# Attention for batches 1 to 3: the two heads' 64-token tiles packed into one 128-partition tile

## The chip, the cores and the metric

One core of a Trainium2 chip runs the whole program. The metric is the device time of one execution in microseconds (us); a comparison uses the median of several runs. The core has a matrix engine (TensorE, PE in the profile, its weight loads as PEld), VectorE (DVE), ScalarE (ACT), GpSimd (POOL) and SyncE (SP), which here only issues DMAs.

## The reference

Local causal attention and a memory readout are mixed by a gate, and two dense feed-forward layers follow. Shapes: B=4, H=8, S=576, D=64; tokens x model 2304 x 512, hidden width 2048.

```python
scores = scale * q @ k.T                      # causal mask
a = exp(scores - max); a /= a.sum() + 1e-9
local = a @ v
q_p = phi(q)                                  # where(x > 0, x, exp(x) - 1) + 1
mem_out = (q_p @ M_prev) / (q_p @ z_prev + 1e-6)
attn = g * mem_out + (1 - g) * local          # g = sigmoid(beta), one per head
x = attn as [B*S, H*D]
h = x @ w_in;   y = (s * relu(h)**2 + b) @ w_out
h2 = y @ w_in2; out = (h2 * tanh(softplus(h2))) @ w_out2
```

## The kernel before

The attention is cut into half units. A half unit is one batch, one pair of heads, and either the first 320 tokens (group `TA`) or the last 256 (group `TB`); `pair` emits its steps. There are 4 x 4 x 2 = 32 of them. In front of the 576 tokens stand 64 rows of zeros, so that the padded 640 tokens make five query tiles of 128. Group `TA` has tiles 0, 1 and 2; of tile 0 only 64 rows are real tokens.

For one half unit of `TA` in batches 1 to 3 (twelve of them) `pair` does this:

- SP issues one DMA for q with z (`qn`, or a place in `stage`), one per head for q and k transposed (`qk`), one for M and v (`vx`), and at the end one for the result.
- POOL takes min(q, 0) (L535), ACT the exponential (L536), DVE forms phi(q), its product with z and the sum per head and token (L537 to L539), gates and inverts it (L533, L541).
- PE makes the scores (L571), for each of tiles 0, 1, 2 and each head one matmul with 64 rows of the array, 128 columns of weights and 64, 192 or 320 moving columns. The two heads use the two halves of the rows. They are two steps of the plan: tiles 0 and 1 into one pair of PSUM banks, tile 2 into another.
- DVE adds the mask, takes the row's extreme and writes SBUF (L581, one per tile and head); POOL writes the memory part, phi(q) times the inverse norm, in front of the scores (L592, the same count); ACT takes the exponential with its row sum (L589, the same count).
- DVE gates and inverts the sums (L533, L610), and POOL scales the rows (L607, the same count; `E_NORM[False]` is 'PPPPD' and tiles 0 to 2 are all 'P').
- PE transposes P block by block (L630, 6 blocks a head, 12 in all), ACT copies them to SBUF (L635), and PE multiplies with M and v (L652: 128 rows, 64 weight columns a head, the two heads in the two halves of the columns; 384, 256 and 128 moving columns).
- ACT copies 320 columns out (L666), and SP stores them to `x_d`.

Every fp32 matmul shows as two weight loads and two matmuls in the trace; a transpose shows as one.

The order of all steps on all engines is written by `Plan`, a list scheduler: each step has an engine, a cost and a priority, and the plan simulates the engines with these costs and emits the steps in the order that comes out. Attention steps have priorities from 50 upward (7 more for each half unit) and go ahead of the first feed-forward layer, whose matmuls (L881 and L957, priorities from 500) fill PE's free time. DMAs that put derived weights aside (L825, L866, L868, priority 499) fill SP's. Two sets of input buffers (one in pool `at`, one in `stage`) let one half unit be loaded ahead. PSUM ring `a` has five banks. After the attention come the rest of layer 1 and then the second layer's blocks (L1112, L1185, L1188).

The lines that decide how PE is laid out for the scores and for P times v:

```python
nc.tensor.matmul(ps[k][i].t[:, a:a + hi - lo], qkt(t * P, P)[rows(i)], kt(lo, hi - lo)[rows(i)], start=True, stop=True)   # L571
nc.tensor.matmul(pv.t[rows(i), cols].rearrange("p (t q) -> p t q", q=P), vx()[:, i, c, :], PT[i].t[...], ...)             # L652
```

Of the kernel before, what the change touches and what calls it, by code (L numbers as in the profile page):

```python
# [9 lines left out]
F32 = mybir.dt.float32  # L10
F32R = mybir.dt.float32r
BF16 = mybir.dt.bfloat16
I32 = mybir.dt.int32
U32 = mybir.dt.uint32
AF = mybir.ActivationFunctionType
ALU = mybir.AluOpType
# [3 lines left out]
P = 128  # L20
MASKED = -1.0e30
HUGE = 3.0e38
TRUNC = -0.5 + 2.0 ** -13 - 2.0 ** -15
PE, ACT, DVE, POOL, DMA = range(5)
# [29 lines left out]
def act_us(n, extra=0):  # L54
    return 0.094 + 0.00083 * n + 0.093 * extra


def dve_us(n, fast=False):
    return 0.068 + (0.00052 if fast else 0.00104) * n


def pool_us(n):
    return 0.3 + 0.0013 * n
# [6 lines left out]
def two(s):  # L70

    s.two = True
    return s
# [119 lines left out]
class Plan:  # L193
# [29 lines left out]
    def add(self, engine, us, prio, f, r=(), w=(), after=(), keep=(), share=1.0):  # L223


        bufs = list({id(b): b for b in (*r, *w, *keep) if b.ring is not None}.values())
        new = [b for b in bufs if b.maker is None]
        waits = {id(s): s for b in r for s in b.writers}
        waits.update((id(s), s) for s in after)
        s = Step(engine, us, prio, f, list(waits.values()), bufs, new)  # L230
        s.share = share
        s.left = len(waits)
        for x in waits.values():
            x.next.append(s)
        for b in bufs:
            b.users += 1
            if b.maker is None:
                b.maker = s
            elif id(b.maker) not in waits:
                b.maker.next_start.append(s)  # L240
                s.left += 1
        for b in w:
            b.writers.append(s)
        self.steps.append(s)
        return s
# [114 lines left out]
def attention_then_two_ffn(ctx: ExitStack, tc: tile.TileContext, qk, qz, vm, beta,  # L360
# [3 lines left out]
    nc = tc.nc  # L364
    B, H = qk.shape[:2]
    NQ, D = qz.shape[3] - 1, qz.shape[4]
    SP = NQ * P
    S = SP - D
# [16 lines left out]
    SCALE = 1.0 / float(D) ** 0.5  # L385
    TA, TB = groups_all = tuple(range(3)), tuple(range(3, NQ))
    NONE = 5
    plan = Plan()
    add = plan.add
# [6 lines left out]
    ident = const.tile([P, P], F32, name="ident")  # L396
    make_identity(nc, ident)
    mask = const.tile([P, SP], BF16, name="mask")
# [3 lines left out]
    igate = const.tile([P, 2, H], F32, name="igate")  # L402
    sb = const.tile([P, 2], F32, name="sb")

    x_d = dram.tile([P, NCC, NT], F32, name="x_d")
# [9 lines left out]
    x_in = {(b, g): Buf() for b in range(B) for g in range(2)}  # L415
# [21 lines left out]
    small, att = ExitStack(), ExitStack()  # L437
    m1s = small.enter_context(tc.tile_pool(name="m1s", bufs=1))
    at = att.enter_context(tc.tile_pool(name="at", bufs=1, side="right"))
    m1t, m2a, m2c = [], [], []  # L440

    R = {}
# [22 lines left out]
    attention_steps = []  # L465
# [3 lines left out]
    def pair(b, p, prio, g, place=None, apart=False):  # L469
# [4 lines left out]
        def add(engine, us, f, r=(), w=(), keep=(), share=1.0):  # L474
            attention_steps.append(plan.add(engine, us, prio, f, r, w, keep=keep, share=share))
            return attention_steps[-1]
# [190 lines left out]
        c0 = b * S + q0  # L667
        add(DMA, 0.7, lambda: nc.sync.dma_start(x_d[:, p, c0:c0 + m], xs.t[:, :m]), [xs], [x_in[b, groups_all.index(g)]])


    W = {}

# [584 lines left out]
    n = len(plan.steps)  # L1257
# [3 lines left out]
    for x, a in zip(("qk", "qn", "vx"), (0, 832, 1344)):  # L1261
        R[x].homes(stage, [a], conversion_left)
    for b, p, g, prio in halves_[H:]:
        pair(b, p, prio, g)
    R["c1"] = Ring("c1").homes(stage, [2048 + 256 * i for i in range(4)], conversion_left).more(m1s, 1, conversion_left)
    c1_steps = {"in": {r: [] for r in range(NR)}, "out": {r: [] for r in range(NR)}}
    for r in range(NR):
# [23 lines left out]
    order1, n = [], 0  # L1291
    for i in range(len(seq)):
        order1.append((i, True))
        for k in range(n, len(seq)):
# [3 lines left out]
            n = k + 1  # L1298
    for i, begins in order1:
# [3 lines left out]
        if begins:  # L1303
# [5 lines left out]
            m = len(plan.steps)  # L1309
            halves[i] = first(j, fcs, at_, -1.0)  # L1310
            in_steps[fcs[0] // FPR] += [x for x in plan.steps[m:] if x.engine == PE]
        else:
            y_part(part, fcs, accs[part], *halves.pop(i), at_ + 0.01)
            out_steps[fcs[0] // FPR] += plan.steps[m0:]
            m = len(plan.steps)
# [18 lines left out]
    n = len(plan.steps)  # L1334
# [26 lines left out]
    n = len(plan.steps)  # L1361
# [76 lines left out]
```

## Time and profile before

| | |
|---|---|
| median of 3 runs | 956.82 us (955.77 to 958.04) |
| the profiled execution's own time | 956.4 us |
| its span, first to last instruction | 954.6 us |
| PE busy | 937.3 us, 98% |
| DVE, ACT, POOL busy | 776.0, 641.5, 220.7 us |
| granted TensorE clock | 1.00 nearly throughout |

The chain of work that ended last follows each step back to what released it. A busy share is an average over stages; the stretches show which engine binds where. Attention of batches 1 to 3 runs from about 77 to 311 us.

### The profile page before, as it was taken

The page shows a single profiled execution, that of the slowest core. Times are in us where ns is not written, and L with a number is a line of the kernel's source. Part 1 is how long each engine was busy: PE and PEld are TensorE (multiplying, and loading weights), DVE is VectorE, ACT ScalarE, POOL GpSimd, SP SyncE. Part 2 cuts the span into 40 slices and gives each one's busy share as a digit, 9 for nine tenths or more (in the row PEclk, how much of TensorE's full clock was granted, in tenths as well). Part 3 has the DMA queues.
Part 4 walks back from the last instruction along what each step waited for, and adds up shares of the span by engine and source line. Part 5 has one row for each costly group of instructions (what it writes and reads, how often), then busy time and mean ns, then how long its engine had stood idle before and what let it go on. Part 6 is the DMA issues. An engine that isn't in the chain of part 4 may idle for free.

```text
span 954.6 us, 19318 instructions
## 1 busy us (share of the span) xinstructions
PE 937.3 (98%) x6594; PEld 862.0 (90%) x6594; DVE 776.0 (81%) x1886; ACT 641.5 (67%) x1393; POOL 220.7 (23%) x377
## 2 busy tenths in 40 slices
PE   7899999999999999999999999999999999999998
PEld 6677788878788999888899999999999999999998
DVE  6999989899978787568658998889957799577874
ACT  6899878777777476889757865557634476344652
POOL 4635445577663000000023400000000000000000
PEclk9999999999999999999999999999999999999999
DMA  9976757999996789988885658885786655775545
GB/s 236 311 201 176 235 162 224 266 267 265 283 257 198 221 282 308 291 301 274 291 289 165 206 184 266 303 278 177 234 285 218 209 163 191 259 226 199 170 139 178
DMA packets 148339, 224.11 MB, mean 235 GB/s; under 512 B 15120, under 2 KB 122640, under 8 KB 141328
## 3 DMA queue, kind: packets, MB, share of 16 engines
q1 hardware_dynamic: 141408, 174.63, 59.4%
q0 software_dynamic: 6688, 48.24, 15.3%
q8 instruction: 52, 0.85, 0.4%
q14 instruction: 47, 0.39, 0.1%
q10 hardware_dynamic: 144, 0.00, 0.0%
HBM read 159.39 MB, written 63.44 MB: 233 GB/s over the span
## 4 chain that ended last, share of the span: by engine, by line
PE 79%; DVE 4%; ACT 2%; DMA 1%; issue 1%; POOL 0%; DVEq 0%; POOLq 0%
PE bank L1112 20%; PE bank L1185 19%; PE bank L881 12%; PE bank L957 12%; PE bank L1188 5%; PE bank L652 4%; PE bank L630 4%; PE bank L571 3%; DMA stage<-wi_sums_d 1%; DVE S L740 1%; DMA qn<-in_qz 0%; DVE g L1118 0%; DVE woh L740 0%; POOL Pt L607 0%; DVE g L1150 0%
## 5 line engine op out<-in xcount | busy, mean ns | idle before, releaser
L1112 PE MATMUL bank<-wi,woh 128*128 128x384 f32 x477 | 112.5, 334 | 0.0
L1112 PE MATMUL bank<-wi,wol 128*128 128x384 f32 x483 | 105.9, 335 | 0.8 <-DVE wil L1118 0.6
L1185 PE MATMUL bank<-wol,S 128*128 128x256 f32 x756 | 102.3, 283 | 0.0
L1185 PE MATMUL bank<-woh,S 128*128 128x256 f32 x756 | 101.9, 283 | 0.0
L1185 PEld LDWEIGHTS bank<-wol,S 128*128 128x128 f32 x756 | 96.2, 192 | 0.0
L1185 PEld LDWEIGHTS bank<-woh,S 128*128 128x128 f32 x756 | 95.9, 192 | 0.0
L1112 PEld LDWEIGHTS bank<-wi,wol 128*128 128x128 f32 x483 | 85.6, 188 | 1.6 <-DVE wil L1118 0.9
L1112 PEld LDWEIGHTS bank<-wi,woh 128*128 128x128 f32 x477 | 85.2, 188 | 0.4
L589 ACT ACTIVATE Pt<-Pt,mx 128x64 f32<-128x64 f32 (+4 forms) x152 | 82.6, 564 | 1.8 <-DVE mx L581 1.8
L635 ACT COPY PT<-bank 128x384 f32<-128x384 f32 (+2 forms) x160 | 68.2, 491 | 22.4 <-PE bank L630 15.0
L607 POOL TENSOR_SCALAR Pt<-Pt,rs 128x448 f32<-128x448 f32 (+3 forms) x100 | 65.7, 676 | 39.2 <-DVE rs L610 26.8
L592 POOL TENSOR_SCALAR Pt<-ex,nm 128x64 f32<-128x64 f32 x152 | 60.2, 419 | 63.1 <-DVE nm L541 35.4
L630 PE MATMUL bank<-ident,Pt 128*128 128x128 f32 x444 | 62.5, 275 | 6.1 <-DVE Pt L607 1.7
L630 PEld LDWEIGHTS bank<-ident,Pt 128*128 128x128 f32 x444 | 49.5, 140 | 11.2 <-issue 3.4
L581 DVE CUSTOM_DVE_ANT_0 Pt<-bank,mask 128x64 f32<-128x64 f32 (+3 forms) x152 | 50.5, 373 | 8.0 <-PE bank L571 5.7
L739 ACT CAST woh<-stage 128x1024 fp32r<-128x1024 f32 (+2 forms) x42 | 37.2, 885 | 27.4 <-PE bank L1112 17.9
L740 DVE TENSOR_TENSOR woh<-stage,woh 128x1024 fp32r<-128x1024 f32 (+2 forms) x42 | 42.7, 1018 | 13.8 <-ACT woh L739 13.7
L1125 POOL TENSOR_SCALAR woh<-woh,sb 128x384 f32<-128x384 f32 (+1 forms) x6 | 5.5, 916 | 183.3 <-ACT woh L1124 183.3
L739 ACT CAST S<-g 128x384 fp32r<-128x384 f32 x56 | 28.7, 513 | 27.2 <-PE bank L1185 19.2
L1092 POOL DMA_DIRECT2D woh<-wo_split_d x13 | 6.9, 530 | 156.2 <-DVE g L1150 76.4
L881 PE MATMUL bank<-xh,wi 128*128 128x256 f32 x256 | 42.5, 292 | 0.0
L957 PE MATMUL bank<-gl,woh 128*128 128x256 f32 x256 | 41.5, 288 | 0.0
(331 smaller groups left out, 2491.1 us busy)
## 6 DMA issues: line engine op xcount, KB each, us to landing
woh<-wo_split_d POOLq DMA_DIRECT2D x13, 1024.0 KB, 5.6
wol<-wi_split_d POOLq DMA_DIRECT2D x12, 1024.0 KB, 5.2
wol<-wo_split_d POOLq DMA_DIRECT2D x11, 1024.0 KB, 5.2
stage<-in_w_in SPq DMA_DIRECT2D x21, 512.0 KB, 5.6
stage<-in_w_out SPq DMA_DIRECT2D x19, 512.0 KB, 4.7
stage<-wi_d SPq DMA_DIRECT2D x24, 384.0 KB, 5.1
stage<-wo_d SPq DMA_DIRECT2D x18, 512.0 KB, 3.7
wo_split_d<-high SPq DMA_DIRECT2D x32, 256.0 KB, 4.6
```

What stands on the lines that cost most here:

```text
L581: nc.vector.tensor_tensor_reduce(at_t(i, t, D + lo, D + hi), x.t[:, a:a + hi - lo], mask[:, SP - w + lo:SP - w + hi], -SCALE, mx.t[:, i, t ...
L589: nc.scalar.activation(at_t(i, t, D, w + D), at_t(i, t, D, w + D), AF.Exp, bias=mx.t[:, i, t + k:t + k + 1], scale=-1.0, accum_out=rs.t[:, ...
L592: add(POOL, 0.33, lambda i=i, t=t: nc.gpsimd.tensor_scalar(at_t(i, t, 0, D), ex.t[:, i, t - lo_t, :], nm.t[:, i, t - lo_t:t - lo_t + 1], 1 ...
L607: (nc.vector if e == DVE else nc.gpsimd).tensor_scalar(x, x, r, *((None, ALU.mult) if e == DVE else (1.0, ALU.mult, ALU.mult)))
L630: nc.tensor.transpose(ps.t[:, x, :], at_t(i, t, c * P, (c + 1) * P), ident)
L635: (nc.vector.tensor_copy if dve else nc.scalar.copy)(PT[i].t[:, x:x + n], ps.t[:, :n])
L739: lambda: (nc.scalar.copy if e == ACT else nc.vector.tensor_copy)(t[0](0), src()), r, [t[2], half], after)
L740: lo = two(add(DVE, dve_us(n), prio, lambda: nc.vector.tensor_tensor(t[0](1), src(), t[0](0).bitcast(F32), op=ALU.subtract), [*r, half], [ ...
L881: nc.tensor.matmul(ph, w_at(nm, r, cc)[:, o:o + P], x_at(x, cc), start=(begin and part == 0 and cc == 0), stop=(part == 2 and cc == NCC - ...
L957: nc.tensor.matmul(acc[ec // per].t[:, (ec % per) * n:(ec % per + 1) * n], w_at(nm, fc // FPR, fc % FPR)[:, ec * P:(ec + 1) * P], t(x)[:, ...
L1112: nc.tensor.matmul(ps.t[:, :H2], w[i // 4].t[:, j, kk, at_], x[kk].t[:, k], start=begin and part == kk == 0, stop=part == 2 and kk == 1, s ...
L1185: nc.tensor.matmul(acc[t].t[:, :DH], s.t[:, j, t * P:(t + 1) * P], x.t[:, k, q % 4], start=q == part == 0, stop=q == NQ2 - 1 and part == 2)
```

## The change

The twelve half units of `TA` in batches 1 to 3 go to a new function, `leading`, in place of `pair`. It leaves out the 64 zero rows: the 64-token tiles of both heads become slot 0, one tile of 128 partitions (head 0 in partitions 0 to 63, head 1 in 64 to 127), and slots 1 to 4 are the two full tiles of each head. So there are five tiles where there were six. The scores are one step in three banks; slot 0's two matmuls take 64 rows and 64 weight columns each, and the six matmuls are issued in a new order. q and z come in four DMAs where there was one. P has 11 blocks to transpose, and P times M for slot 0 is a matmul of 64 moving columns a head. At the start three DVE copies and two GpSimd copies fill two small tables, `gates` and `step_`. `pair` still does all other half units.

```diff
+    gates = at.tile([P, 2, H // 2, 5], F32, name="gates")
+    nc.vector.tensor_copy(gates[:, :, :, 1:]..., igate...to_broadcast([P, H, 2, 2]))
+    step_ = at.tile([P, D], BF16, name="step")
+    for i in range(2):
+        x = slice(D * i, D * i + D)
+        nc.vector.tensor_copy(gates[x, :, :, 0], igate[x, :, i::2])
+        nc.gpsimd.tensor_copy(step_[x], mask[x, SP - P + D * i:SP - P + D * i + D])
...
+    def leading(b, p, prio):
+        n_q, n_s = 320, 5
+        slots = ((0, 64), *((q, w, i) for i in range(2) for q, w in ((64, 192), (192, 320))))
...
+        add(DMA, 0.5, lambda: nc.sync.dma_start(zq(4, 4)..., qz[b, hs, :, 2:4]...), w=[q_in])
+        for i in range(2):
+            add(DMA, 0.15, lambda i=i: nc.sync.dma_start(q_in.t[rows(i), :6 * D]...[:, :, 0], qz[b, 2 * p + i, D:, 0:2]), w=[q_in])
+        add(DMA, 0.25, lambda: nc.sync.dma_start(zq(1, 2), qz[b, hs, :, 0]...), w=[q_in])
...
+        for a, n in ((0, 1), (1, 4)):       # the product with z, in two instructions
...
+        bank = [Buf(R["a"], [P, 512]) for _ in range(3)]
+        where = [(2, 0), (0, 320), (0, 0), (1, 320), (1, 0)]
+        def mm():
+            for s, i in ((0, 0), (4, 1), (2, 0), (0, 1), (1, 0), (3, 1)):
+                (q0, w), (x, a), full = slots[s][:2], where[s], s > 0
+                nc.tensor.matmul(bank[x].t[:, a:a + w] if full else bank[x].t[rows(i), a:a + w],
+                                 qk_in.t[rows(i), q0:q0 + (P if full else D)], qk_in.t[rows(i), n_q:n_q + w],
+                                 start=True, stop=True, skip_group_check=not full)
+        add(PE, 0.03 + 576 * 0.00167, mm, [qk_in], bank, [*Pt, mx, rs], 1.0)
...
+        for s in (0, 1, 3, 2, 4):           # mask and extreme (DVE), memory part (POOL), exponential (ACT)
...
+        for s in (0, 1, 3, 2, 4):           # scaling, all on POOL
+            add(POOL, pool_us(w), lambda s=s, w=w: nc.gpsimd.tensor_scalar(...), ...)
...
+        for x, o, blocks in ((0, 0, [(0, 0), (1, 0), (1, 1)]), (1, 0, [(3, 0), (3, 1)]),
+                             (0, 3, [(2, c) for c in range(3)]), (1, 2, [(4, c) for c in range(3)])):
...
+            for c, k in ((0, 0), (0, 1), (1, 1), (2, 1)):    # P times M and v; k == 0 is slot 0, 64 columns
...
-        pair(b, p, prio, g)
+        if g == TA:
+            leading(b, p, prio)
+        else:
+            pair(b, p, prio, g)
```

## Rows read from the trace of the kernel before

**Rows 1.** The page's busy times, and the chain's shares by engine.
```profile
PE 937.3 (98%) x6594; PEld 862.0 (90%) x6594; DVE 776.0 (81%) x1886; ACT 641.5 (67%) x1393; POOL 220.7 (23%) x377
...
PE 79%; DVE 4%; ACT 2%; DMA 1%; issue 1%; POOL 0%; DVEq 0%; POOLq 0%
```

**Rows 2.** Busy us by stretch: PE, PEld, DVE, ACT, POOL; clock, DMA share, GB/s.
```profile
100.00:150.00 50.00, 47.47 (x384) 39.62 (x383) 46.00 (x134) 40.49 (x99) 25.61 (x39) 1.00 0.65 191
150.00:200.00 50.00, 49.95 (x407) 40.69 (x406) 43.72 (x146) 38.45 (x111) 29.58 (x55) 1.00 0.91 258
...
500.00:550.00 50.00, 49.06 (x279) 47.80 (x277) 45.90 (x88) 40.44 (x79) 20.05 (x20) 1.00 0.58 185
```

**Rows 3.** The chain of waits, 283 to 296 us: start, length, what.
```profile
283.88 0.47 PE bank L957 x4
...
285.15 1.29 PE bank L571 x12
286.44 1.45 PE bank L652 x12
287.89 0.67 PE bank L957 x4
288.56 1.97 PE bank L630 x18
```

**Rows 4.** Timeline of PE, 76.5 to 81.5 us: scores of one half unit in two groups.
```profile
77.04 0.82 PE L571 MATMUL bank<-qk 64*128 64x64 f32 x8
77.79 0.73 PE L881 MATMUL bank<-xl,wi 128*128 128x256 f32 x4
78.45 0.81 PE L571 MATMUL bank<-qk 64*128 64x320 f32 x4
79.19 2.17 PE L652 MATMUL bank<-PT,wih 128*64 128x256 f32 x20
```

**Rows 5.** Timeline of PE and its weight loads, narrow stretches around 285 to 287 us.
```profile
285.74 0.70 PE L571 MATMUL bank<-qk 64*128 64x320 f32 x4
...
286.01 0.44 PE L571 MATMUL bank<-qk 64*128 64x320 f32 x2
...
286.37 0.14 PEld L652 LDWEIGHTS bank<-PT,vx 128*64 128x64 f32 x2 [0.44 <-issue]
...
286.37 0.20 PEld L652 LDWEIGHTS bank<-PT,vx 128*64 128x64 f32 x4 [0.44 <-issue]
```

**Rows 6.** Groups by line and shape, 140 to 312 us: busy us, mean ns.
```profile
L592 POOL TENSOR_SCALAR Pt<-ex,nm 128x64 f32<-128x64 f32 x94 | 34.4, 389 | 32.9 <-DVE nm L541 17.9 <-PE bank L571 5.9 <-DVE nm L533 3.9
...
L607 POOL TENSOR_SCALAR Pt<-Pt,rs 128x64 f32<-128x64 f32 x20 | 9.7, 500 | 18.0 <-DVE rs L610 14.2 <-ACT Pt L589 2.8 <-ACT xs L666 1.0
...
L589 ACT ACTIVATE Pt<-Pt,mx 128x64 f32<-128x64 f32 x18 | 6.5, 384 | 0.0
...
L581 DVE CUSTOM_DVE_ANT_0 Pt<-bank,mask 128x64 f32<-128x64 f32 x37 | 7.3, 217 | 3.3 <-PE bank L571 3.1 <-POOL Pt L592 0.2
```

**Rows 7.** Timeline of DVE and of POOL, 6.3 to 9.5 us.
```profile
8.18 0.69 DVE L717 SCALAR_TENSOR_TENSOR stage<-stage 128x512 int32<-128x512 int32 x1 [0.93 <-ACT stage L713]
...
7.66 1.18 POOL L535 TENSOR_SCALAR ex<-wih 128x384 f32<-128x384 f32 x1 [4.30 <-DMA wih<-in_qz]
```

**Rows 8.** Timeline of SP's queue, 193 to 204 us: DMA issues.
```profile
197.08 0.44 SPq L514 DMA_DIRECT2D stage<-in_qz  x1
197.62 0.45 SPq L516 DMA_DIRECT2D qn<-in_qz  x1
...
198.64 0.46 SPq L866 DMA_DIRECT2D wi_resident_d<-wi  x1
```

**Rows 9.** Who waited for whom, 50 to 320 us: us in total, times, longest.
```profile
POOL ex L535 <- DMA qn<-in_qz: 8.8, 4, 4.2
```

**Rows 10.** Timeline of PE where the second layer begins: idle us before, releaser.
```profile
504.78 0.44 PE L1112 MATMUL bank<-wi,wol 128*128 128x384 f32 x1 [0.59 <-DVE wil L1118]
...
550.72 0.81 PE L1188 MATMUL bank<-S,woh 128*128 128x384 f32 x3 [0.82 <-DVE S L740]
```

More of the change, by code (lines that the diff above doesn't have):

```diff
@@ L439, in attention_then_two_ffn @@
     at = att.enter_context(tc.tile_pool(name="at", bufs=1, side="right"))
+    gates = at.tile([P, 2, H // 2, 5], F32, name="gates")
+    nc.vector.tensor_copy(gates[:, :, :, 1:].rearrange("p k a (h t) -> p (k a) h t", t=2),
+                          igate.rearrange("p k (a h) -> p (k a) h", h=2).unsqueeze(3).to_broadcast([P, H, 2, 2]))
+    step_ = at.tile([P, D], BF16, name="step")
[3 more added lines that the diff above has]
+        nc.gpsimd.tensor_copy(step_[x], mask[x, SP - P + D * i:SP - P + D * i + D])
     m1t, m2a, m2c = [], [], []
@@ L668, in pair, with add, rows, zq @@
         add(DMA, 0.7, lambda: nc.sync.dma_start(x_d[:, p, c0:c0 + m], xs.t[:, :m]), [xs], [x_in[b, groups_all.index(g)]])
+    def leading(b, p, prio):
+        def add(engine, us, f, r=(), w=(), keep=(), share=1.0):
+            attention_steps.append(plan.add(engine, us, prio, f, r, w, keep=keep, share=share))
+            return attention_steps[-1]
+        hs = slice(2 * p, 2 * p + 2)
+        n_q, n_s = 320, 5
+        slots = ((0, 64), *((q, w, i) for i in range(2) for q, w in ((64, 192), (192, 320))))
+        qk_in, q_in, v_in = Buf(R["qk"], [P, 2 * n_q]), Buf(R["qn"], [P, 8 * D]), Buf(R["vx"], [P, 6 * D])
+        def rows(i):
+            return slice(D * i, D * i + D)
+        def zq(a, n):
+            return q_in.t[:, a * D:(a + n) * D].rearrange("p (s d) -> p s d", d=D)
+        def q_all():
+            return zq(3, 5)
+        add(DMA, 0.5, lambda: nc.sync.dma_start(zq(4, 4).rearrange("p (h t) d -> p h t d", t=2), qz[b, hs, :, 2:4].rearrange("h p a d -> p h a d")), w=[q_in])
+        for i in range(2):
+            add(DMA, 0.15, lambda i=i: nc.sync.dma_start(q_in.t[rows(i), :6 * D].rearrange("p (k s d) -> p k s d", k=2, d=D)[:, :, 0],
+                                                         qz[b, 2 * p + i, D:, 0:2]), w=[q_in])
+        add(DMA, 0.25, lambda: nc.sync.dma_start(zq(1, 2), qz[b, hs, :, 0].rearrange("h p d -> p h d")), w=[q_in])
+        for i in range(2):
+            add(DMA, 0.0009 * 2 * n_q, lambda i=i: nc.sync.dma_start(
+                qk_in.t[rows(i)].rearrange("p (a n) -> p a n", a=2),
+                qk[b, 2 * p + i, rows(i)][:, D:][:, :2 * S].rearrange("p (a n) -> p a n", a=2)[:, :, :n_q]), w=[qk_in])
+        ex = Buf(R["ex"], [P, n_s, D])
+        nm, mx, rs = (Buf(R[x], [P, 16]) for x in ("nm", "mx", "rs"))
+        n_e = n_s * D
+        def gate(x, k, eps):
+            nc.vector.scalar_tensor_tensor(x, x, eps, gates[:, k, p], op0=ALU.add, op1=ALU.mult)
+        add(POOL, 0.3 + 0.0032 * n_e, lambda: nc.gpsimd.tensor_scalar_min(ex.t, q_all(), 0.0), [q_in], [ex])
+        add(ACT, act_us(n_e), lambda: nc.scalar.activation(ex.t, ex.t, AF.Exp), [ex], [ex])
+        two(add(DVE, dve_us(n_e), lambda: nc.vector.scalar_tensor_tensor(ex.t, q_all(), 0.0, ex.t, op0=ALU.max, op1=ALU.add), [ex, q_in], [ex]))
+        for a, n in ((0, 1), (1, 4)):
+            def weigh(a=a, n=n):
+                x, y, z = zq(3 + a, n), ex.t[:, a:a + n], zq(0, 1)
+                if a:
+                    x, y = (u.rearrange("p (h t) d -> p h t d", t=2) for u in (x, y))
+                    z = zq(1, 2).unsqueeze(2).to_broadcast([P, 2, 2, D])
+                nc.vector.tensor_tensor(x, y, z, op=ALU.mult)
+            two(add(DVE, dve_us(n * D), weigh, [ex, q_in], [q_in]))
+        add(DVE, dve_us(n_e), lambda: nc.vector.tensor_reduce(nm.t[:, :n_s], q_all(), axis=mybir.AxisListType.X, op=ALU.add), [q_in], [nm])
+        add(DVE, 0.15, lambda: gate(nm.t[:, :n_s], 0, 1e-6), [nm], [nm])
+        add(DVE, 0.09, lambda: nc.vector.reciprocal(nm.t[:, :n_s], nm.t[:, :n_s]), [nm], [nm])
+        Pt = [Buf(R["Pt0"], [P, P]), *(Buf(R[f"Pt{t}"], [P, P * (t + 1)]) for _ in range(2) for t in (1, 2))]
+        Pt_in, mx_in, rs_in = ([Buf() for _ in slots] for _ in range(3))
+        bank = [Buf(R["a"], [P, 512]) for _ in range(3)]
[7 more added lines that the diff above has]
+        add(PE, 0.03 + 576 * 0.00167, mm, [qk_in], bank, [*Pt, mx, rs], 1.0)
+        attention_steps[-1].mode = 1
+        for s in (0, 1, 3, 2, 4):
+            w, (x, a) = slots[s][1], where[s]
+            def least(s=s, w=w, x=x, a=a):
+                m = mask[:, SP - w:] if s else step_
+                nc.vector.tensor_tensor_reduce(Pt[s].t[:, D:D + w], bank[x].t[:, a:a + w], m, -SCALE, HUGE, ALU.add, ALU.min, mx.t[:, s:s + 1])
+            add(DVE, 0.14 + 0.00105 * w, least, [bank[x]], [Pt_in[s], mx_in[s]], [Pt[s], mx])
+            add(POOL, 0.33, lambda s=s: nc.gpsimd.tensor_scalar(Pt[s].t[:, :D], ex.t[:, s], nm.t[:, s:s + 1], 1.0, op0=ALU.mult, op1=ALU.mult),
+                [ex, nm], [Pt_in[s]], [Pt[s]])
+            add(ACT, 0.28 + 0.00083 * w, lambda s=s, w=w: nc.scalar.activation(
+                Pt[s].t[:, D:D + w], Pt[s].t[:, D:D + w], AF.Exp, bias=mx.t[:, s:s + 1], scale=-1.0, accum_out=rs.t[:, s:s + 1]),
+                [Pt_in[s], mx_in[s]], [Pt_in[s], rs_in[s]], [Pt[s], mx, rs])
+        gated, done = Buf(), Buf()
+        add(DVE, 0.15, lambda: gate(rs.t[:, :n_s], 1, 1e-9), rs_in, [gated], [rs])
+        add(DVE, 0.09, lambda: nc.vector.reciprocal(rs.t[:, :n_s], rs.t[:, :n_s]), [gated], [done], [rs])
+        for s in (0, 1, 3, 2, 4):
+            w = slots[s][1]
+            add(POOL, pool_us(w), lambda s=s, w=w: nc.gpsimd.tensor_scalar(
+                Pt[s].t[:, D:D + w], Pt[s].t[:, D:D + w], rs.t[:, s:s + 1], 1.0, ALU.mult, ALU.mult), [done, Pt_in[s]], [Pt_in[s]], [Pt[s], rs])
+        PT = [Buf(R["PT"], [P, 9, P]) for _ in range(2)]
+        for x, o, blocks in ((0, 0, [(0, 0), (1, 0), (1, 1)]), (1, 0, [(3, 0), (3, 1)]),
+                             (0, 3, [(2, c) for c in range(3)]), (1, 2, [(4, c) for c in range(3)])):
+            ps, n = Buf(R["a"], [P, 4, P]), len(blocks)
+            def turn(ps=ps, blocks=blocks):
+                for y, (s, c) in enumerate(blocks):
+                    nc.tensor.transpose(ps.t[:, y], Pt[s].t[:, c * P:c * P + P], ident)
+            add(PE, 0.01 + 0.109 * n, turn, [Pt_in[s] for s in sorted({s for s, _ in blocks})], [ps], [PT[x], *(Pt[s] for s, _ in blocks)])
+            add(ACT, act_us(n * P) - 0.04, lambda x=x, o=o, n=n, ps=ps: nc.scalar.copy(PT[x].t[:, o:o + n], ps.t[:, :n]), [ps], [PT[x]])
+        pv, xs = Buf(R["a"], [P, 512]), Buf(R["xs"], [P, 320])
+        def mm():
+            for c, k in ((0, 0), (0, 1), (1, 1), (2, 1)):
+                for i in range(2):
+                    y = pv.t[rows(i)]
+                    if k == 0:
+                        dest, src = y[:, :D], PT[0].t[:, 0, rows(i)]
+                    elif c < 2:
+                        dest, src = y[:, D:n_q].rearrange("p (t q) -> p t q", t=2), PT[i].t[:, 1 - i + c:4 - i + c:2]
+                    else:
+                        dest, src = y[:, 192:n_q], PT[i].t[:, 5 - i]
+                    nc.tensor.matmul(dest, v_in.t.rearrange("p (h t d) -> p h t d", h=2, d=D)[:, i, c], src,
+                                     start=k == 0, stop=k == 0 or c == 2, skip_group_check=k > 0)
+        add(DMA, 0.75, lambda: nc.sync.dma_start(v_in.t.rearrange("p (h t d) -> p h t d", h=2, d=D), vm[b, hs, :, :3].rearrange("h p a d -> p h a d")), w=[v_in])
+        add(PE, 0.04 + 704 * 0.00167, mm, PT + [v_in], [pv])
+        attention_steps[-1].mode = 2
+        add(ACT, act_us(n_q) - 0.04, lambda: nc.scalar.copy(xs.t, pv.t[:, :n_q]), [pv], [xs])
+        add(DMA, 0.7, lambda: nc.sync.dma_start(x_d[:, p, b * S:b * S + n_q], xs.t), [xs], [x_in[b, 0]])
@@ L1263, in attention_then_two_ffn @@
     for b, p, g, prio in halves_[H:]:
-        pair(b, p, prio, g)
+        if g == TA:
+            leading(b, p, prio)
+        else:
+            pair(b, p, prio, g)
     R["c1"] = Ring("c1").homes(stage, [2048 + 256 * i for i in range(4)], conversion_left).more(m1s, 1, conversion_left)
```

## The prediction

> **What bounds the kernel now.** I read the page first, then the busy time by stretch, the chain of waits, and PE's timeline inside one half unit. The page says PE is busy 98% of the span and the chain lies on PE for 79% [rows 1]. That is an average, so the stretches decide. While the changed half units run, PE is busy 49.95 of 50 us, DVE 43.72, ACT 38.45 and POOL 29.58 [rows 2]. The chain there is matmul after matmul, with attention groups and filler alternating [rows 3]. The filler (layer 1, L881 and L957) is always waiting behind the attention, so a microsecond more or less of PE work in a half unit moves the end by itself, and a microsecond on DVE, ACT or POOL does not. After 311 us the rest of layer 1 follows on PE. Only around 500 to 550 us do others hold it up, by 0.59 and 0.82 us in two places [rows 10].
>
> **What one half unit costs PE now.** Its scores (L571) take 1.29 us, P times v (L652) 1.45 us, and 18 transposes of a neighbouring unit 1.97 us, 0.11 us each [rows 3]. In the scores the two heads run side by side: four matmuls of 320 columns span 0.70 us and the second pass starts 0.27 us after the first (285.74 to 286.01), so a pass costs 0.84 ns a column for both heads together [rows 5]. The last pass would be through at 286.28, but the next shape (`128*64` after `64*128`) starts at 286.37: a change of shape costs 0.09 us of emptying [rows 5]. Rows 4 give the full price, since there the scores of one unit were issued in two groups with filler between: 0.75 us (77.04 to 77.79) and 0.74 us (78.45 to 79.19), 1.49 us against 1.29 us [rows 3, 4]. One more group costs 0.20 us. It is visible in the second group: two passes of 0.27 us make 0.54 us, and 0.20 us remain, 0.09 us of emptying and 0.11 us of a first weight load that nothing hides [rows 4, 5]. With 64 weight columns that load is shorter: the second pair of loads in L652 ends 0.06 us after the first (0.20 against 0.14) [rows 5]. A change in the number of columns alone pays too: filler after L652 (`128*128` after `128*64`) takes 0.67 us for four matmuls against 0.47 us elsewhere [rows 3].
>
> **The change on PE, part by part.**
>
> P times v: 704 moving columns instead of 768, two passes each, 2 x 64 x 0.84 ns = 0.11 us less. The two new matmuls have the shape of their neighbours, so they empty nothing.
>
> Transposes: 11 for 12, 0.11 us less.
>
> Scores: 576 columns a head as before, but slot 0's two matmuls use 64 rows and 64 weight columns, and all others 64 rows and 128. The issue order is slot 0 of head 0, two of 320 columns, slot 0 of head 1, two of 192 columns. If a change of shape empties the array here as in the rows, one group becomes four. Slot 0 alone: first load 0.06, two passes at the load's 0.06, emptying 0.09, together 0.27 us, twice. The pair of 320 columns: 0.74 us as in rows 4. The pair of 192 columns: 2 x 0.16 + 0.20 = 0.52 us. Sum 1.80 us against 1.29 us: 0.51 us more [rows 3 to 5].
>
> No row holds a `64*64` matmul, so this term is bounded from both sides. Below: no emptying, each head streams its 576 columns beside the other, and slot 0's weights load faster (0.06 for 0.11, two passes), 0.10 us less than now. Above: three more groups at the full 0.20 us, and slot 0's passes no longer beside the other head's (2 x 0.11), 0.82 us more. I take 0.51: the change of columns alone in rows 3 is the nearest case, and it pays.
>
> [...]
>
> Sum a unit: 0.51 - 0.11 - 0.11 = 0.29 us, times twelve 3.5 us. Two of the twelve units have their scores in two groups now (the one of rows 4 and one more); as the scores become one step, they get back 0.20 us each. That leaves 3.1 us more.
>
> **The change elsewhere, and what hides it.** One tile fewer saves a unit 0.39 and 0.50 us on POOL (L592, L607), 0.38 us on ACT (L589) and 0.22 us on DVE (L581), and 64 of 384 columns in the phi steps [rows 6]; the split product adds one short DVE instruction. All of it lies beside a full PE [rows 2], so I put it at nothing; were PE not full there, the 0.89 us of POOL would be the most it could give. POOL scaled these tiles before too. The three DVE copies at the start fit into the 0.93 us in which DVE waits before 8.18 us, and the two of GpSimd into its 4.30 us [rows 7]; uncovered they would cost some 0.5 us once. Scores in one step need three free banks of five at once, where two and two did; if a bank is late, PE's queue stands, filler included. What frees one is the 0.22 us DVE read or a copy on ACT, so up to 0.2 us a unit, 2.6 us in all, a part of the upper end.
>
> DMAs: three more a unit, each 0.44 to 0.46 us of SP's queue [rows 8], 1.4 us a unit, 36 DMAs and some 16 us in all. SP issues nearly without a break there; behind them stand the other loads, the results' stores and the put-aside weights (L866), which can go later. I cost it at nothing: a unit is loaded one ahead, and POOL waited for q four times, 8.8 us in all [rows 9], while PE had filler.
>
> **The time.** 956.4 + 3.1 = 959.5 us for the profiled execution; the runs' median lies 0.4 us above that execution, so 959.9 us.
>
> **Rivals.**
>
> No emptying between `64*64` and `64*128`. For it: the heads do run independently in rows 5. Against it: every change of shape that the trace has pays. Then a unit saves 0.10 + 0.11 + 0.11 = 0.32 us, twelve 3.8, and 0.4 of the two split units: 952.6, median 953.0 us, faster. It decides from the point where the scores cost less than 1.29 + 0.22 us.
>
> Half the price. The array empties but the next weights are already in: the groups cost 0.27, 0.63, 0.21 and 0.41, 1.52 us, and a unit comes out even; with the split units 956.4 us. The same class holds where the two stalls of rows 10 (1.4 us) take up part of the delay because DVE is ahead: 958.5 us. For it: DVE and ACT get lighter. Against it: the 0.11 us load stands exposed in rows 4.
>
> SP's queue becomes a wait. If q arrives 1.4 us later for each unit and PE ran out of filler, all of it would show, 16.8 us; with filler present perhaps a quarter, 4 us on top: 964 us. Against it: rows 2, PE full at a DMA share of 0.91; in 100 to 150 us, where waits for loads did reach PE, it lost 2.5 us.
>
> **Chances.** Four groups at the rows' price 0.58, no emptying 0.20, half price or taken up 0.17, SP's queue 0.05. For the likeliest alone I give 957.8 to 962.5 us (the order of all steps is planned anew, which moves waits by one or two us either way). The whole range reaches to the fast rival and to the upper bounds in part: 953.0 to 963.0 us. A difference under 0.2%, 1.9 us, is about what a measurement of this kernel cannot tell from none. Faster: nearly all of the no-emptying case, 0.20. Same: the half price and the low edge of the likeliest, 0.23. Slower 0.57.
>
> **What would show it.** The scores of a changed unit at 1.8 us in the chain, with gaps between slot 0 and its neighbours, would show the main step right; 1.2 us with slot 0's matmuls starting within nanoseconds of the 320-column ones would show it wrong. P times v should fall to 1.34 us, transposes to 11 a unit. POOL busy should fall by about 11 us with the end unmoved by it. Waits of POOL for q well above 8.8 us would point to SP. I am wrong if the array takes both shapes at once.

## The result

The changed kernel takes 968.84 us (median of 6, 966.80 to 971.28), the kernel before 957.43 us beside it: ratio 1.0122, 95% interval 1.0103 to 1.0140, about 11 us slower. The forecast was 959.9 us with a range up to 963.0. The sign was right; the loss is nearly four times the 3.1 us forecast.

The profiled execution (967.49 us) has a span of 965.7 us, 11.1 us more than before. The page's busy times and the chain's shares by engine:

```profile
PE 944.2 (98%) x6630; PEld 866.2 (90%) x6630; DVE 774.5 (80%) x1877; ACT 635.0 (66%) x1369; POOL 205.8 (21%) x355
...
PE 84%; DMA 4%; DVE 4%; ACT 4%; issue 2%; SPq 1%; POOL 1%; DVEq 0%; ACTq 0%; POOLq 0%
```

Against [rows 1], POOL's busy time fell by 14.9 us (about 11 us were forecast), and it bought nothing. PE is busy 6.9 us longer. The chain of work that ended last now runs over DMA and ACT for 8% of the span where it was 3%. By stretch (PE, PEld, DVE, ACT, POOL; clock, DMA share, GB/s):

```profile
116.00:120.00 4.00, 4.00 (x24) 4.00 (x23) 4.00 (x18) 2.80 (x6) 2.99 (x5) 0.57 0.68 201
150.00:200.00 50.00, 49.81 (x411) 40.64 (x410) 42.12 (x137) 38.03 (x107) 27.16 (x54) 1.00 0.79 224
250.00:300.00 50.00, 45.96 (x364) 34.83 (x361) 39.06 (x143) 34.39 (x102) 28.92 (x54) 0.93 0.87 248
266.00:274.00 8.00, 5.83 (x31) 3.36 (x32) 4.62 (x17) 3.51 (x9) 2.06 (x2) 0.57 0.97 301
...
266.00:270.00 4.00, 1.83 (x7) 0.85 (x8) 2.04 (x4) 3.25 (x8) 2.06 (x2) 0.57 0.87 244
```

From 150 to 200 us PE is as full as in [rows 2]. From 250 to 300 us it is not: PE is idle for 4.0 us, and the granted clock is 0.57 in eight of the microseconds (266 to 274), 0.50 in six of them (267 to 273). A part of that stretch falls into PE's idle time (266 to 270 us: PE is busy for 1.83 of 4 us) and costs nothing more. What it costs PE's work is read from two groups below: 2.4 us. Around 118 us (116 to 120) PE is busy throughout at 0.57, and the lower clock costs 0.43 x 4 = 1.7 us, an estimate from these two numbers.

**The predicted step.** PE and its weight loads in one changed half unit; L740 makes the scores, L792 multiplies P with M and v (start, length, line, operation, shape):

```profile
285.88 0.19 PEld L740 LDWEIGHTS bank<-qk 64*64 64x64 f32 x2
...
286.14 0.30 PEld L740 LDWEIGHTS bank<-qk 64*128 64x128 f32 x4
...
286.88 0.19 PEld L740 LDWEIGHTS bank<-qk 64*64 64x64 f32 x2 [0.44 <-issue]
...
287.13 0.30 PEld L740 LDWEIGHTS bank<-qk 64*128 64x128 f32 x4
...
287.66 1.42 PE L792 MATMUL bank<-PT,vx 128*64 128x64 f32 x16
```

The four groups last 0.26, 0.74, 0.25 and 0.53 us, 1.78 us in all; the prediction had 0.27, 0.74, 0.27 and 0.52. The chain gives P times v 1.35 us (predicted 1.34):

```profile
285.95 1.77 PE bank L740 x12
287.73 1.35 PE bank L792 x16
```

**Where the rest went.** The chain of waits, 259 to 272 us:

```profile
259.28 0.26 SPq L699
...
259.60 6.11 DMA xr<-x_d
...
265.72 0.02 ACT xh L1033
...
267.86 0.27 ACT PT L778
...
268.17 3.18 PE bank L740 x12
271.35 2.37 PE bank L792 x16
```

Read it backwards: a unit's scores (L740) wait for a bank, the bank for a copy of PT on ACT (L778), the copy stands behind a cast of layer 1's x (L1033), and the cast waits for the load of x, which took 6.1 us. SP's queue shows what the load stood behind and among (L699, L701 and L703 are q and z of one unit, L1032 is the load of x):

```profile
258.07 0.42 SPq L795 DMA_DIRECT2D vx<-in_vm  x1
258.59 0.48 SPq L799 DMA_DIRECT2D x_d<-xs  x1
259.17 0.37 SPq L699 DMA_DIRECT2D stage<-in_qz  x1
259.60 1.06 SPq L1032 DMA_DIRECT2D xr<-x_d  x2
260.70 1.25 SPq L701 DMA_DIRECT2D stage<-in_qz  x2
262.00 0.59 SPq L703 DMA_DIRECT2D stage<-in_qz  x1
```

q and z of the unit take 0.37 + 1.25 + 0.59 = 2.2 us of SP where one DMA took 0.44 us [rows 8]. No gap between these issues is over 0.1 us: SP has no time left, and whatever stands in its queue is issued late. ACT stands still meanwhile, 4.32 us:

```profile
261.22 0.19 ACT L597 ACTIVATION_READ_ACCUMULATOR Pt<-Pt,mx 128x1 f32 x1
265.72 0.62 ACT L1033 CAST xh<-xr 128x512 fp32r<-128x512 f32 x1 [4.32 <-DMA xr<-x_d]
```

PE then starts the scores after 3.98 us of idling (PE's timeline):

```profile
268.17 3.18 PE L740 MATMUL bank<-qk 64*64 64x64 f32 x12 [3.98 <-ACT PT L778]
```

It starts at the lower clock (0.50 from 268 to 272 us): by the chain the scores take 3.18 us for 1.77, and P times v 2.37 for 1.35, together 2.4 us more. Who waited for whom, 50 to 320 us (us in total, times, longest):

```profile
ACT xh L1033 <- DMA xr<-x_d: 5.1, 3, 4.3
...
POOL ex L543 <- DMA qn<-in_qz: 4.9, 4, 2.4
...
POOL ex L716 <- DMA stage<-in_qk: 3.3, 1, 3.3
...
POOL ex L716 <- DMA qn<-in_qz: 1.6, 1, 1.6
...
POOL ex L716 <- DMA stage<-in_qz: 1.4, 1, 1.4
```

POOL's wait for q, which the prediction would have watched, hardly changed: L543 belongs to the half units that `pair` still does, L716 to the changed ones, and the waits for q are 7.9 us together against 8.8 us in [rows 9] (11.2 with the 3.3 us that are put down to a load from `in_qk`). It was x that came late for ACT, a load that the change does not touch.

### The profile page after: what moved, and what is told of

The parts are those of the page before. It is cut to its first block, busy times and chain, and to the rows that moved or that the text cites. A ratio compares the mean times of both kernels' runs of the same rounds, so it can differ in the third digit from the quotient of the medians.

```text
span 965.7 us, 19382 instructions
## 1 busy us (share of the span) xinstructions
PE 944.2 (98%) x6630; PEld 866.2 (90%) x6630; DVE 774.5 (80%) x1877; ACT 635.0 (66%) x1369; POOL 205.8 (21%) x355
## 4 chain that ended last, share of the span: by engine, by line
PE 84%; DMA 4%; DVE 4%; ACT 4%; issue 2%; SPq 1%; POOL 1%; DVEq 0%; ACTq 0%; POOLq 0%
PE bank L1242 23%; PE bank L1315 19%; PE bank L1011 13%; PE bank L1087 12%; PE bank L1318 5%; PE bank L638 2%; PE bank L740 2%; PE bank L660 2%; PE bank L579 2%; DMA xr<-x_d 2%; PE bank L792 2%; PE bank L775 1%; ACT PT L643 1%; DMA stage<-in_w_out 1%; ACT Pt L756 1%
## 5 line engine op out<-in xcount | busy, mean ns | idle before, releaser
L1242 PEld LDWEIGHTS bank<-wi,woh 128*128 128x128 f32 x525 | 92.9, 188 | 0.6
L1242 PEld LDWEIGHTS bank<-wi,wol 128*128 128x128 f32 x435 | 78.1, 188 | 1.0 <-DVE wol L1248 0.4
L643 ACT COPY PT<-bank 128x512 f32<-128x512 f32 (+2 forms) x112 | 45.9, 497 | 12.5 <-PE bank L638 12.0
L597 ACT ACTIVATE Pt<-Pt,mx 128x448 f32<-128x448 f32 (+4 forms) x80 | 51.0, 645 | 1.8 <-DVE mx L589 1.8
L638 PE MATMUL bank<-ident,Pt 128*128 128x128 f32 x300 | 39.8, 275 | 4.2 <-DVE Pt L615 2.1
L1087 PE MATMUL bank<-gh,woh 128*128 128x256 f32 x256 | 41.3, 287 | 0.0
L1087 PE MATMUL bank<-gh,wol 128*128 128x256 f32 x256 | 41.1, 286 | 0.0
L869 ACT CAST wol<-stage 128x1024 fp32r<-128x1024 f32 (+2 forms) x32 | 28.5, 889 | 19.1 <-PE bank L1242 16.5
L638 PEld LDWEIGHTS bank<-ident,Pt 128*128 128x128 f32 x300 | 33.2, 141 | 8.2 <-issue 2.7
```

The costliest lines, as they stand in the source:

```text
L597: nc.scalar.activation(at_t(i, t, D, w + D), at_t(i, t, D, w + D), AF.Exp, bias=mx.t[:, i, t + k:t + k + 1], scale=-1.0, accum_out=rs.t[:, ...
L638: nc.tensor.transpose(ps.t[:, x, :], at_t(i, t, c * P, (c + 1) * P), ident)
L643: (nc.vector.tensor_copy if dve else nc.scalar.copy)(PT[i].t[:, x:x + n], ps.t[:, :n])
L869: lambda: (nc.scalar.copy if e == ACT else nc.vector.tensor_copy)(t[0](0), src()), r, [t[2], half], after)
L1087: nc.tensor.matmul(acc[ec // per].t[:, (ec % per) * n:(ec % per + 1) * n], w_at(nm, fc // FPR, fc % FPR)[:, ec * P:(ec + 1) * P], t(x)[:, ...
L1242: nc.tensor.matmul(ps.t[:, :H2], w[i // 4].t[:, j, kk, at_], x[kk].t[:, k], start=begin and part == kk == 0, stop=part == 2 and kk == 1, s ...
```

## The experiments

Three theories are to be told apart. "PE": the shapes alone make the loss. "Loads": SP's added issues make loads of x late. "New order": the replanned order of steps makes it, without the DMAs. Each kernel ran beside the kernel before; the ratio is to that one. Unless said otherwise the plan is fed the same steps and costs as in the kernel it starts from, so that the order of steps is unchanged.

**Slot 0 with 128 weight columns.**

```diff
-                nc.tensor.matmul(bank[x].t[:, a:a + w] if full else bank[x].t[rows(i), a:a + w],
-                                 qk_in.t[rows(i), q0:q0 + (P if full else D)], ...
+                x, a = (x, a) if full or not i else (1, 320)
+                nc.tensor.matmul(bank[x].t[:, a:a + w], qk_in.t[rows(i), q0:q0 + P], ...
```

> Theories. PE: the changes of shape in the scores cost 0.49 us a unit (1.78 against 1.29), 5.9 us over twelve units; with the savings of P times v and the transposes some 3 us of the 11 are PE work. Loads: the three more q DMAs a unit push back the loads of x that ACT's casts wait for in order; the banks come late, PE stands, and its granted clock falls afterwards; some 8 us. New order: neither; the whole order was planned anew with costs that do not fit, and the two stalls (1.75 us at 114, 3.98 us at 264) come from the place of steps, not from the DMAs. This kernel is the changed one in the same order of steps, but slot 0's two matmuls use 128 weight columns like the others (head 1's first 64 tokens of batches 1 to 3 then get wrong scores: part of the computation is changed). PE: scores at 1.29 to 1.34 us, about 5.5 us faster than the changed kernel, 963. Loads and new order: the same 5.5 us for this part, with both stalls and both stretches at the lower clock still there. If the stalls go too (957 or less), it was PE's delay that made them.

964.24 us, ratio 1.0070 (1.0051 to 1.0088): 4.6 us less than the changed kernel. The chain has the scores at 1.29 us again:

```profile
281.65 1.29 PE bank L741 x9
```

By who waited for whom, 50 to 320 us, the waits for x are still there:

```profile
ACT xh L1033 <- DMA xr<-x_d: 4.3, 3, 2.0
```

So the shapes cost 0.49 us a unit (5.9 us over twelve; the time fell by 4.6). ACT still waits for x and PE for ACT without them, though less: PE's longest wait for a copy of PT before the scores is 1.6 us here, against 3.98.

**One DMA for q and z, in rows of 2 KB.**

```diff
-        add(DMA, 0.5, lambda: nc.sync.dma_start(zq(4, 4)..., qz[b, hs, :, 2:4]...), w=[q_in])
...
+        add(DMA, 0.5, lambda: nc.sync.dma_start(zq(0, 8), ql[b, p]), w=[q_in])
+        for us in (0.15, 0.15, 0.25):
+            add(DMA, us, lambda: None, w=[q_in])
```

> The changed kernel with the same order of steps, but each of the twelve units' q and z come in one DMA from a host layout (2 KB a partition) where four came (256 and 512 bytes a piece). Loads: SP and the queues get back what they lost, the casts at 264 us don't wait 4 us, the stalls and the lower clock go: about 961 (956.4 + 3.1 + what is left). PE alone: 968.8, no change. New order: within 2 us of 968.8, since the order is the same.

959.92 us, ratio 1.0026 (1.0016 to 1.0037): 8.9 us come back. What is left, 2.4 us above the kernel before beside it (957.57), is near the prediction's 3.1. The page's busy times:

```profile
PE 940.6 (98%) x6630; PEld 865.2 (90%) x6630; DVE 775.4 (81%) x1877; ACT 635.1 (66%) x1369; POOL 205.3 (21%) x355
```

The stretch in which the changed kernel had its stall:

```profile
250.00:300.00 50.00, 49.94 (x421) 39.45 (x419) 42.71 (x152) 38.11 (x109) 28.13 (x53) 1.00 0.87 255
```

The timeline of ACT, the same cast:

```profile
260.53 0.60 ACT L1033 CAST xh<-xr 128x512 fp32r<-128x512 f32 x1
```

The timeline of SP, with the load of x for that cast:

```profile
253.36 1.02 SPq L1032 DMA_DIRECT2D xr<-x_d  x2
...
254.93 0.48 SPq L525 DMA_DIRECT2D qn<-in_qz  x1
256.61 1.13 SPq L532 DMA_DIRECT2D stage<-in_qk  x2
```

In the same order of steps SP has time to spare (255.41 to 256.61). x is issued 7.2 us before ACT comes to its cast; in the changed kernel it was 1.8 us (259.60 to 261.41). PE loses nothing in this stretch and the clock stays at 1.00. PE's busy time and the span (957.9 us) are each 3.3 us above before: the PE part of the prediction by itself. The order is that of the changed kernel, so the new-order theory falls.

**One DMA, in 1024 pieces of 256 bytes.**

```diff
-        add(DMA, 0.5, lambda: nc.sync.dma_start(zq(0, 8), ql[b, p]), w=[q_in])
+        add(DMA, 0.5, lambda: nc.sync.dma_start(zq(0, 8), ql[b, p].rearrange("s p d -> p s d")), w=[q_in])
```

> As the kernel before it in this list, one DMA a unit in the same order, but from a layout that makes it 1024 pieces of 256 bytes (the changed kernel has 768 of 256 and 512). If the time of SP's issues delays the loads of x, this runs like the one DMA of 2 KB rows (about 961). If the small pieces in the DMA queues delay them, it runs like the changed kernel or worse (969). New order: 968 either way.

960.30 us, ratio 1.0025 (1.0010 to 1.0040), as with 2 KB. The number of issues counts here, not the size of the pieces: those of 256 bytes cost nothing that shows (960.30 us against 959.92).

**The kernel before with four DMAs.**

```diff
+    nc.sync.dma_start(x[:, :, 2:], src[:, :, 2:])
+    for i in range(2):
+        nc.sync.dma_start(x[:, i, 1], src[:, i, 1])
+    nc.sync.dma_start(x[:, :, 0], src[:, :, 0])
```

> The kernel before in its own order of steps, but q and z of the twelve half units of 320 tokens in batches 1 to 3 are loaded by four DMAs (two tiles of both heads, the first tile of each head, z) where one stood. Loads: slower by 2 to 8 us (959 to 965), with waits of ACT's casts for x and perhaps a stretch at the lower clock. PE and new order: within 1 us of 957.4.

962.65 us, ratio 1.0050 (1.0034 to 1.0067). The loss appears with no other part of the change, by the same chain at another place. The same number of added issues costs 5.1 us here and 8.9 us in the changed kernel; what makes the difference was not separated. The timelines of ACT and of PE, the cast and PE's next step:

```profile
241.25 0.62 ACT L903 CAST xh<-xr 128x512 fp32r<-128x512 f32 x1 [3.40 <-DMA xr<-x_d]
...
243.43 2.83 PE L652 MATMUL bank<-PT,vx 128*64 128x384 f32 x12 [2.85 <-ACT PT L635]
```

The clock in that stretch:

```profile
242.00:250.00 8.00, 6.57 (x33) 5.06 (x34) 5.72 (x24) 3.92 (x9) 2.08 (x7) 0.57 0.87 247
```

The profiled execution is the longest of four (964.57 us, mean granted clock 0.996; the others 961.91 to 963.01 us at 0.998 to 1.000): most of the loss comes with little or no time at the lower clock.

**Fewer added DMAs in the kernel before.** Two DMAs, one for each head; then three:

```diff
+    for i in range(2):
+        nc.sync.dma_start(x[:, i], src[:, i])
```

> The kernel before in its own order, with two DMAs for q and z of a unit (one for each head) where one stood: a third of the added issues of the run with four (5.1 us slower). In proportion: 1.7 us slower, 959. With a threshold: within 1 us of 957.

957.61 us, ratio 1.0007 (0.9997 to 1.0016).

```diff
+    nc.sync.dma_start(x[:, :, 2:], src[:, :, 2:])
+    for i in range(2):
+        nc.sync.dma_start(x[:, i, :2], src[:, i, :2])
```

> The kernel before in its own order, with three DMAs for q and z of a unit (two tiles of both heads; z and the first tile of each head). One more DMA a unit cost nothing that shows (ratio 1.0007), three more 5.1 us. In proportion to the third: 960 to 961. If the loss sets in where a load of x comes later than ACT's cast stands, two more may lie on either side: under 958.5 (not yet there) or about 961 to 962 (there), and in the second case the trace has a wait of a cast for x above 2 us and a stop of PE behind it.

959.97 us, ratio 1.0032 (1.0018 to 1.0046). With 12, 24 and 36 added DMAs the time rises by 0.7, 3.1 and 4.8 us. The first step is nearly free and the second is not, but the intervals are too wide to call it a threshold. With three DMAs the longest wait and the stop behind it are shorter than with four. Who waited for whom, 60 to 320 us:

```profile
ACT xh L903 <- DMA xr<-x_d: 6.2, 3, 2.3
```

The timeline of PE:

```profile
240.37 1.52 PE L652 MATMUL bank<-PT,vx 128*64 128x384 f32 x12 [1.24 <-ACT PT L635]
```

**The added DMAs issued by GpSimd.**

```diff
-            ... nc.sync.dma_start(q_in.t[rows(i), :6 * D]...
+            ... nc.gpsimd.dma_start(q_in.t[rows(i), :6 * D]...
```

(The one of z likewise.)

> The changed kernel in its order of steps, but the three added DMAs of a unit are issued by GpSimd and not by SP; the pieces in the queues are the same. SP's issue time: the loads of x land as in the kernel with one DMA, about 960. Number of DMAs or pieces in the queues, whoever issues them: 967 to 969. GpSimd's own steps come some 1.5 us later per unit and it has room (busy 206 of 966 us); if they become the wait, 963 to 966.

962.68 us, ratio 1.0063 (1.0048 to 1.0078): between the two. ACT's wait for x is gone, with the changed kernel's pieces in the queues; so it was SP's time. The group of the casts (busy us, mean ns, idle before):

```profile
L1033 ACT CAST xh<-xr 128x512 fp32r<-128x512 f32 x10 | 6.2, 622 | 0.5 <-DMA xr<-x_d 0.5
```

What remains above the single DMA is 2.8 us. GpSimd is busy for 230.2 us where it was 205.8, and PE's timeline has a wait late in the second layer:

```profile
716.27 1.31 PE L1242 MATMUL bank<-wi,woh 128*128 128x384 f32 x6 [1.40 <-DMA woh<-wi_split_d]
```

The clock is at 0.72 in six microseconds (0.28 x 6 = 1.7 us by estimate):

```profile
116.00:122.00 6.00, 5.85 (x36) 5.72 (x36) 6.00 (x22) 4.63 (x10) 5.50 (x9) 0.72 0.65 199
```

Whether the move to GpSimd causes these two was not tried; the lower clock stands behind a stop of 1.8 us that the other kernels have too (last section). What moved is 0.6 us of SP an issue (0.62 for each of L701's two, 0.59 for L703, in the unit shown above), and it decided: 962.68 us for 968.84.

**The plan told that x lands 3 us later.**

```diff
-            add(DMA, 0.002 * n * per, prio, lambda ...: nc.sync.dma_start(xr.t, x_d[...]), need, [xr])
+            add(DMA, 0.002 * n * per, prio, lambda ...: nc.sync.dma_start(xr.t, x_d[...]), need, [xr]).lag = 0.0 if big else 3.0
```

> The changed kernel with all its DMAs, but the plan that writes the order of steps is told that the loads of x land 3 us later, so that ACT's casts come behind the copies of PT which they held up. If the loss is a cast in the wrong place of ACT's order: both waits for x fall under 1 us and the time goes to 960 to 962. If SP's lack of time costs wherever the casts stand (the next load is then the late one): 965 to 969. Any new order moves the time by 1 or 2 us either way.

968.96 us, ratio 1.0124 (1.0105 to 1.0142), no better than the changed kernel. The plan writes another order. The casts hardly wait any longer; now q is the late one, and PE stops behind it (1.8 us at 266 us, the longest such stop). Who waited for whom, 50 to 320 us:

```profile
POOL ex L543 <- DMA qn<-in_qz: 17.0, 7, 4.6
...
ACT xh L1033 <- DMA xr<-x_d: 0.6, 1, 0.6
```

In this order, moving the cast only chose who waits.

**Slot 0's second matmul moved to the end of the scores** (from the kernel with one DMA):

```diff
-            for s, i in ((0, 0), (4, 1), (2, 0), (0, 1), (1, 0), (3, 1)):
+            for s, i in ((0, 0), (4, 1), (2, 0), (1, 0), (3, 1), (0, 1)):
```

> The kernel with one DMA of q and z a unit (959.9 us, same order of steps), in which the second of slot 0's two matmuls goes from the middle of the scores to their end, so that the scores are three groups of one shape and not four. Price by change of shape (my terms: 0.20 us a group): scores 1.58 to 1.60 us for 1.78, twelve units 2.2 to 2.4 us, about 957.6. If a 64-column group costs only its own passes and its place does not matter: 959.9, no change.

958.40 us, ratio 1.0012 (1.0002 to 1.0022), by PE's timeline 1.58 us for the scores:

```profile
277.45 1.64 PE L740 MATMUL bank<-qk 64*64 64x64 f32 x12
279.03 1.42 PE L792 MATMUL bank<-PT,vx 128*64 128x64 f32 x16
```

One group fewer saves 0.20 us a unit; PE busy falls from 940.6 to 938.4 us.

**Slot 0 as one block-diagonal matmul** (from the kernel with one DMA; q, k and the block in one DMA):

```diff
...
-            for s, i in ((0, 0), (4, 1), (2, 0), (0, 1), (1, 0), (3, 1)):
...
+            for s, i in ((0, 0), (4, 1), (2, 0), (3, 1), (1, 0)):
+                (q0, w), (x, a), k = slots[s][:2], where[s], rows(i) if s else slice(P)
+                q0 += D if s else 0
+                nc.tensor.matmul(bank[x].t[:, a:a + w], qk_in.t[k, q0:q0 + P], qk_in.t[k, D + n_q:D + n_q + w], start=True, stop=True)
```

> The kernel with one DMA of q and z a unit and the same order of steps, and slot 0's scores as one matmul of 128 rows: its weights are a 128x128 block of the host's layout with head 0's q and head 1's q on the diagonal and zeros elsewhere, in the filler's shape; q, k and that block come in one DMA where two came. PE: the scores are one group of four matmuls of one shape, 1.25 to 1.30 us; with 0.11 us each of P times v and the transposes a unit costs 0.2 us less PE time than before the change, 2.4 us in all: 953.5 to 955.5, faster than the kernel before. If SP's issues were only shifted and the stalls come with the order: 958 or more.

952.61 us, ratio 0.9958 (0.9943 to 0.9973): faster than both kernels. PE is busy 2.6 us less than before (the page):

```profile
PE 934.7 (98%) x6606; PEld 864.2 (91%) x6606; DVE 774.7 (81%) x1877; ACT 634.5 (67%) x1369; POOL 207.7 (22%) x355
```

The scores take 1.33 us (PE's timeline, 257.62 to 258.95):

```profile
257.62 1.40 PE L741 MATMUL bank<-qk 128*128 128x64 f32 x10
258.95 1.42 PE L792 MATMUL bank<-PT,vx 128*64 128x64 f32 x16
```

In the profiled executions the span falls by 2.8 us (951.8 for 954.6), nearly all of it PE's work; the medians differ by 4.3 us, and the rest of that stays open.

**The same with a plan of its own** (two DMA steps where the plan had six):

```diff
+        add(DMA, 1.0, lambda: nc.sync.dma_start(zq(0, 8), ql[b, p]), w=[q_in])
+        add(DMA, 1.15, lambda: nc.sync.dma_start(qk_in.t, qkl[b, p]), w=[qk_in])
```

> The kernel with the block matmul and the single DMAs once more, but the plan knows it has one DMA each for q with z and for q, k, and writes an order of its own. If the order of steps matters little once SP has time: 951.5 to 953.5, as in the changed kernel's order. If the 952.6 were luck of that order: 955 or more.

954.11 us (950.38 to 954.75), ratio 0.9958 (0.9943 to 0.9972). The median lies between the two figures that were expected, but the ratio is that of the kernel in the other order: the gain is not luck of one order.

**Two DMAs fewer in the other twelve half units too:**

```diff
+            add(DMA, 0.8, lambda: nc.sync.dma_start(part(qn_b, 1, n_t + 1), qb[b, p]) if b else ..., w=[qn_b])
+            add(DMA, 0.3, lambda: b or nc.sync.dma_start(z(), ...), w=[qn_b])
...
+                elif not (b and i):
+                    nc.sync.dma_start(*((qk_b.t[:, :nqc + nkc], qkb[b, p, :, q0_:SP + S]) if b else ...))
```

> The kernel with slot 0's scores as one block matmul and one DMA each for q with z and for q, k (952.6 us, PE busy 934.7, waits of ACT for x near nothing), in the same order of steps, with two DMAs fewer in each of the other twelve half units (q with z in one, both heads' q and k in one). If SP's time costs the same at any load, each DMA fewer gives back what one more cost (5.1 us for 36, so 3.4 us for 24): 949. If it costs only past the point where a load comes late, as I think, there is nothing left to give back: 952 to 953.

954.82 us (951.15 to 956.75), ratio 0.9968 (0.9949 to 0.9987): nothing gained. That agrees with SP's time costing only where a load becomes late.

## Why the prediction was wrong

- Scores, P times v and transposes: right, each group of the scores within 0.02 us, 3.3 us of PE for 3.1 forecast. The rival without emptying is out: 1.78 us against 1.29 with one shape, and 0.20 us for one change of shape. (In that rival's sum 956.4 - 3.8 - 0.4 makes 952.2 and not 952.6 us; nothing hangs on it.) For the pair `64*64` and `64*128`, which no row had, the runs show a price of 0.20 us a group (1.78 us for four groups, 1.58 for three).
- Half price is out: the scores take 1.78 us, not 1.52. That the stalls took up part of the delay does not show in the profiled execution with one DMA, whose span rose by as much as PE (3.3 us); the medians, 2.4 us apart, leave room for a part.
- The step that failed is the DMAs: "I cost it at nothing: a unit is loaded one ahead", with 1.4 us of SP a unit. SP spent 1.75 us more a unit (2.2 against 0.45), and the price was 8.9 us, the difference to the kernel with one DMA. In the profiled executions the kernel with one DMA in 1024 pieces is the plainest to compare with, since its mean granted clock is 1.000 (span 957.1 us, 8.6 less than the changed kernel). Of the 8.6 us, 3.98 are PE's idling at 264 us, 2.4 the lower clock behind it and 1.7 the lower clock around 118 us: 8.1 us. That the last comes from the DMAs is not shown, since the stop before it is in the other kernels too.
- The rival "SP's queue becomes a wait" was the right place at half the price and with a twelfth of the main case's chance. It watched q, which is loaded one ahead, and not the load behind it in SP's queue; so the sign that it named, POOL's waits for q well above 8.8 us, was no guide to the loss. The list of what stands behind the added DMAs named the other loads, but did not follow x to ACT, whose cast stands in order ahead of PT's copies.
- Of the scores' three banks the prediction wrote that a late bank stops PE's queue, filler included. That is what happened, but once for 3.98 us, because of ACT's cast, and not by 0.2 us a unit.
- "PE full at a DMA share of 0.91" [rows 2] was no evidence. It speaks of the transfers; what ran short was SP's time to issue them in order.

## What to carry to other kernels

Count the added DMA issues on the queue that issues them, and follow every load behind them to the engine whose order of steps will wait for it: the full matmul engine here hid a late load only until one of its banks hung on ACT, and then stood for 3.98 us. Before splitting a load, lay the data out so that one DMA suffices (worth 8.9 us here). Where packing two tiles into one makes a new matmul shape, a block of zeros that keeps a shape in use can be cheaper than the smaller matmul (here 1.33 us for the scores against 1.78).

## What the runs showed of the hardware

In the changed kernel a stop of PE cost a good part of its own length once more: around the stop of 3.98 us (264.2 to 268.2) the granted clock was 0.57 from 266 to 274 us. It fell while PE still stood (0.77 from 266 to 267 us, 0.50 from 267 to 268) and was still at 0.50 when PE started again, and PE's work behind it took 2.4 us longer. After a shorter stop it went either way. PE's timeline in the changed kernel:

```profile
115.41 1.33 PE L1011 MATMUL bank<-xh,wi 128*128 128x256 f32 x8 [1.75 <-DVE rt L1069]
```

The same step in the kernel with one DMA:

```profile
115.93 1.22 PE L1011 MATMUL bank<-xh,wi 128*128 128x256 f32 x8 [1.67 <-DVE rt L1069]
```

And that kernel's stretch around it:

```profile
112.00:120.00 8.00, 6.33 (x51) 5.78 (x51) 8.00 (x25) 7.96 (x23) 6.83 (x11) 1.00 0.66 191
```

Behind the first stop stands 0.57 (116 to 120 us), by estimate 1.7 us lost; behind the second 1.00. Nine kernels with the changed attention show this stop, 1.6 to 1.8 us long. In three of them a lower clock follows: the changed kernel (0.57), the one with GpSimd's DMAs (0.72 from 116 to 122 us) and the one with a plan of its own (0.72 from 114 to 120 us). In two it is 1.00 (112 to 120 us): the one with one DMA and the one with the block-diagonal matmul.

A smaller DMA took SP longer to issue in the unit shown above: 0.37 us for L699, but 0.62 us for each of L701's two, which move a quarter of its bytes each (32 and 128 KB).
